# Sink attention and a mixture of attention experts in one program: three more rows are turned by way of DRAM, and the whole order is made anew

## The chip, the core and the metric

The program runs on one core of one Trainium2 chip. The core has a matrix engine (TensorE, here PE), a vector engine (DVE), a scalar engine (ACT), a general engine (POOL) and a queue engine (SP). They share an on-chip memory of 128 partitions (SBUF); PE writes into eight banks of PSUM. Each engine takes its own instructions in order and waits for others by semaphores. The metric is device time of one execution in microseconds (us). Before the change it is 361.75 us, the median of three runs (361.44 to 361.85).

## The reference

```python
def _attn_ref(q, k, v, n_sink, window):        # 4 batches, 8 heads, 768 positions, 64 wide
    scores = scale * np.matmul(q, k.transpose(0, 1, 3, 2))
    keep = is_sink | in_window                 # 4 first keys, and the last 128
    scores = np.where(keep, scores, -1e9)
    ...                                        # softmax over keys
    return np.matmul(a, v)

def _moe_ref(x, w_gate, wq, wk, wv, wo):       # x: heads side by side, 512 wide; 4 experts
    logits = x @ w_gate                        # the best 2 of 4 experts weigh in
    for e in range(E):
        q, k, v = x @ wq[e], x @ wk[e], x @ wv[e]
        scores = np.where(causal, -1e9, scale * (q @ k.transpose(0, 2, 1)))
        ...                                    # softmax over keys
        ye = a @ v @ wo[e]
        ...                                    # out += weight of the expert * ye
```

The first layer is attention in a band with four sinks; the second is full causal attention, once for each expert.

## The kernel before

**Units.** Heads are taken in pairs, and so are experts. A first-layer unit is one pair of heads of one batch (16 units), a second-layer unit one pair of experts of one batch (8 units). The 768 positions are six blocks of 128. Steps are named by batch, pair and layer: `001` is batch 0, pair 0, second layer (the unit of the change), `011` batch 0, pair 1, second layer, and `110` batch 1, pair 1, first layer. First-layer units of one batch are interleaved with the second-layer units of the batch before.

**One row of a second-layer unit.** Row i of six has the queries of block i and i + 1 key blocks. For each it runs: scores on PE (L1385, in `scores`); masking and a running minimum on DVE (L1602); exponentials with their sums on ACT (L1610); the reciprocal of the sum (L1445), times the expert's weight on POOL; scaling of the row (`norm` in `scaled`, L1256 or L1258). Then keys must come onto the partitions before the product with the values, that is, each 128x128 block of the row must be transposed. There are two ways:

- `transposed` (L1463 and following): PE transposes each block in halves of 64 (`turned`, L1457, into two PSUM banks), DVE or ACT copies the result from PSUM to a tile `pt` (`fn` in `evacuate`, L1247 on ACT, L1249 on DVE), and PE forms the product (L1424). Rows of five and six blocks go in two parts. A block takes four transpositions: two experts, two halves.
- `by_way_of_dram` (L1536 and following): the scaled row is written to a tile `u` with its columns rearranged; DVE turns blocks of 32x32 in two instructions (L1547); one DMA writes the tile to a buffer `there` in DRAM (L1550); four DMAs read it back with the blocks in their transposed places (L1554); PE forms the product from `u` (L1424). There are three tiles `u` and four buffers `there`.

`AWAY` names the units and the rows (3, 4 and 5, so rows of four, five and six blocks) that go the second way. In such a unit the rows are taken in the order 4, 5, 2, 3, 0, 1, since the groups of two are taken from the last.

**The order.** No engine's order is written by hand. `Plan.emit` lists all steps, with a cost of its own for each engine that could run the step, and places them one after the other. What stands on PE next follows from a priority (the unit's place, leads such as `WIDE_S`, and for each step a number from the table `NUDGE`), a price for a change of PE's mode (`STAY`, `BULK`) and for waiting (`HURRY`). `ONLY` fixes the engine of steps that could run on two. Loads, writes and reads back go to SP's queue in the same way. Where the planner finds PE without work in the first part of the program, it adds matrix instructions on zeros that nobody reads (`fill`, L1054 and L1057).

Of the kernel before, what the change touches and what calls it, by code (L numbers as in the profile page):

```python
# [34 lines left out]
for other in ("ROWS", "FULL", "cols", "rows"):  # L35
# [783 lines left out]
    "311 store_SPACT 3": SP, "311 fn_DVEACT 20": ACT, "311 fn_DVEACT 21": DVE, "311 store_SPACT 5": SP,  # L819
}  # L820

HURRY = 71.82
STAY = 104.82
BULK = -0.39
# [1197 lines left out]
```

## Time and profile before

| | us |
|---|---|
| median of three runs | 361.75 |
| profiled execution | 361.39 |
| its span, first to last instruction | 359.7 |
| PE busy | 351.2 |
| PE loading weights | 307.1 |
| DVE busy | 290.6 |
| ACT busy | 278.7 |
| POOL busy | 183.2 |

PE is counted in two rows, matrix instructions and loads of weights, which overlap. Its granted clock is 0.998 of full speed over the span, at the higher of its two levels. The page reports 52.05 MB moved by DMA. A busy PE means that some matrix instruction is under way; the gaps between kinds of instructions, in which one ends and the next has not begun to stream, are inside the busy time.

### The profile page before, as it was taken

Reading aid. Unit: us, or ns where it says so; the run is one execution under the profiler, and the core shown is the slowest. Engines: PE = TensorE matmul, PEld = TensorE weight load, DVE = VectorE, ACT = ScalarE, POOL = GpSimd, SP = SyncE. Lnnn points to the kernel's source line nnn. Section 1 sums busy time; section 2 is a strip of 40 time slices with the busy share of each in tenths; the row PEclk is TensorE's granted clock in tenths of the full one; section 3 lists DMA queues with packets and bytes.
Section 4 is the critical chain, followed back from the end, with each engine's and each line's share of the span. In section 5 each row is a group of like instructions: output and inputs, shape, how many; then the busy total and the mean of one; then the engine's idle time right before and its main releaser. Section 6 shows DMA issues by size and latency. Waiting matters only on the chain.

```text
span 359.7 us, 13333 instructions
## 1 busy us (share of the span) xinstructions
PE 351.2 (98%) x4822; PEld 307.1 (85%) x4822; DVE 290.6 (81%) x1263; ACT 278.7 (77%) x985; POOL 183.2 (51%) x432
## 2 busy tenths in 40 slices
PE   8989999999999999999999999999999999999995
PEld 7877789998888889978888888978898889988884
DVE  4899989599979979649799987489699875587951
ACT  2899999299998899758898977489899956056931
POOL 4298999778276764334646550153558600150420
PEclk9999999999999999999999999999999999999999
DMA  7877787943550798329787595029800463059313
GB/s 200 214 178 144 149 165 142 173 77 84 92 87 3 234 263 156 58 88 307 207 159 124 162 283 122 11 87 352 218 7 4 145 223 76 14 201 300 103 58 118
DMA packets 130849, 52.05 MB, mean 145 GB/s; under 512 B 109728, under 2 KB 125088, under 8 KB 130784
## 3 DMA queue, kind: packets, MB, share of 16 engines
q1 hardware_dynamic: 118336, 46.23, 52.0%
q10 hardware_dynamic: 12448, 4.98, 5.3%
q8 instruction: 38, 0.62, 0.8%
q14 instruction: 27, 0.22, 0.2%
HBM read 32.84 MB, written 18.09 MB: 142 GB/s over the span
## 4 chain that ended last, share of the span: by engine, by line
PE 80%; ACT 7%; DMA 4%; DVE 3%; POOL 3%; issue 2%; SPq 0%; ACTq 0%; POOLq 0%; DVEq 0%
PE b L1424 19%; PE b L1839 17%; PE b L1913 10%; PE b L1866 9%; PE b L1385 8%; PE b L1457 7%; PE b L1398 5%; PE b L1380 2%; DMA u<-there 2%; ACT p L1610 2%; PE b L1924 1%; ACT p L1740 1%; DMA there<-u 1%; PE b L1428 1%; DMA vn<-in_v_dram 1%
## 5 line engine op out<-in xcount | busy, mean ns | idle before, releaser
L1610 ACT ACTIVATE p<-p,st 128x256 f32<-128x256 f32 (+5 forms) x96 | 63.6, 665 | 9.8 <-DVE st L1602 9.6
L1740 ACT ACTIVATE p<-p,st 128x132 f32<-128x132 f32 x128 | 51.3, 406 | 3.2 <-DVE st L1736 3.1
L1602 DVE CUSTOM_DVE_ANT_0 p<-b,cmask 128x384 f32<-128x384 f32 (+3 forms) x96 | 45.7, 502 | 1.9 <-PE b L1385 1.5
L1247 ACT ACTIVATE pt<-b 128x256 f32<-128x256 f32 (+3 forms) x101 | 38.5, 419 | 7.5 <-PE b L1457 7.3
L1385 PE MATMUL b<-ks,qs 64*128 64x384 f32 (+3 forms) x384 | 42.2, 338 | 0.0
L1424 PE MATMUL b<-pt,vn 128*64 128x128 f32 x448 | 39.0, 280 | 0.3 <-ACT pt L1247 0.3
L1866 PE MATMUL b<-wvh,x 128*128 128x260 f32 x192 | 36.9, 285 | 0.0
L1440 POOL TENSOR_TENSOR st<-st 128x2 f32<-128x2 f32 (+1 forms) x47 | 9.3, 197 | 52.7 <-ACT p L1610 36.1
L1457 PE MATMUL b<-ident,p 64*128 64x64 f32 x760 | 36.0, 226 | 0.0
L1457 PEld LDWEIGHTS b<-ident,p 64*128 64x128 f32 x760 | 30.4, 138 | 5.4 <-issue 2.5
L1385 PEld LDWEIGHTS b<-ks,qs 64*128 64x128 f32 x384 | 31.6, 186 | 3.3 <-issue 0.7
L1839 PE MATMUL b<-x,wqh 128*128 128x256 f32 (+1 forms) x128 | 32.8, 343 | 0.0
L1839 PE MATMUL b<-x,wkh 128*128 128x256 f32 (+1 forms) x128 | 32.5, 340 | 0.0
L1913 PE MATMUL b<-woh,y 128*128 128x512 f32 x96 | 32.2, 402 | 0.0
L1753 POOL TENSOR_TENSOR p<-p,st 128x528 f32<-128x528 f32 x23 | 24.5, 1066 | 15.0 <-DVE st L1445 10.8
L1547 DVE STREAM_TRANSPOSE u<-u 128x640 f32<-128x640 f32 (+2 forms) x36 | 28.5, 824 | 4.0 <-ACT u L1256 3.7
L1736 DVE CUSTOM_DVE_ANT_0 p<-b,pair_mask 128x132 f32<-128x132 f32 x128 | 31.6, 286 | 0.1
L1679 ACT ACTIVATE p<-p,st 128x256 f32<-128x256 f32 (+1 forms) x64 | 29.1, 460 | 2.9 <-DVE st L1674 2.8
L1866 PEld LDWEIGHTS b<-wvh,x 128*128 128x128 f32 x192 | 30.4, 188 | 0.7 <-issue 0.3
L1249 DVE COPY pt<-b 128x256 f32<-128x256 f32 (+3 forms) x63 | 27.5, 453 | 2.6 <-PE b L1457 2.5
L1424 PEld LDWEIGHTS b<-pt,vn 128*64 128x64 f32 x448 | 25.1, 136 | 4.6 <-issue 1.7
L1866 PE MATMUL b<-wvl,x 128*128 128x260 f32 x96 | 27.1, 282 | 0.0
(133 smaller groups left out, 998.8 us busy)
## 6 DMA issues: line engine op xcount, KB each, us to landing
vn<-in_v_dram SPq DMA_DIRECT2D x24, 192.0 KB, 3.3
kn<-in_k_dram SPq DMA_DIRECT2D x48, 96.0 KB, 2.5
there<-u SPq DMA_DIRECT2D x6, 768.0 KB, 4.8
u<-there SPq DMA_DIRECT2D x24, 192.0 KB, 4.6
...
```

The lines of the kernel that those rows point to most:

```text
L1247: nc.scalar.activation(dst(), src(), AF.Copy)
L1385: nc.tensor.matmul(o, self.qs.t[hs, a, qs], keys(hs, b), start=n == 0, stop=n == 2)
L1424: nc.tensor.matmul(o[e * 64:e * 64 + 64], lhs, rhs, start=e not in self.begun, stop=last and self.done == len(self.steps))
L1457: nc.tensor.transpose(t[g].t[:, n, :], x[gs], ident[gs, gs])
L1602: nc.vector.tensor_tensor_reduce(out=one(e)[:, cs], in0=s2[e].t[:, :(c1 - c0) * 128], in1=mask(c0, c1), scale=times, scalar=st.t[:, 3, es] ...
L1610: nc.scalar.activation(x, x, AF.Exp, bias=st.t[:, 0, es], scale=-1.0, accum_out=st.t[:, 1, es])
L1679: nc.scalar.activation(x, x, AF.Exp, bias=st.t[:, 0, n:n + 1], scale=-1.0, accum_out=st.t[:, 1, n:n + 1])
L1736: nc.vector.tensor_tensor_reduce(out=p.t[:, n, :], in0=s2[e].t[:, 248 * r:248 * r + SW], in1=pair_mask, scale=-scale, scalar=BIG, op0=OP.a ...
L1740: nc.scalar.activation(p.t[:, n, :], p.t[:, n, :], AF.Exp, bias=st.t[:, 0, n:n + 1], scale=-1.0, accum_out=st.t[:, 1, n:n + 1])
L1839: nc.tensor.matmul(t.t, w[a][:, c, es], X[b, c].t[:, x, cs], start=c == 0 and m == 0, stop=c == NCH - 1 and m == 2)
L1866: nc.tensor.matmul(t.t[:, :VW], X[b, c].t[:, a, qs], W["wv"][w][:, c, :], start=c == 0 and n == 0, stop=c == NCH - 1 and n == 2)
L1913: nc.tensor.matmul(t.t, Y[b, c].t[:, a, qs], W["wo"][w][:, c, :], start=c == 0 and n == 0, stop=c == EP - 1 and n == 2)
```

## The change

Unit `001` joins the list `AWAY`, so that seven of the eight second-layer units send rows 3, 4 and 5 by way of DRAM. The tables `NUDGE` and `ONLY` and three numbers of the planner are replaced by others, so the order on every engine is a new one. The rest of the code is unchanged; its line numbers grow by 23 (L1457 becomes L1480, L1424 becomes L1447, L1547 becomes L1570).

```diff
 NUDGE = {
-    "busy_PE": 2.7, " ": -0.4, " busy_PE": 50.2, " busy_PE 0": 4.1, "sink_values_DVE": 20.3, " sink_values_DVE": 16.0,
...
+    "busy_PE": 7.4, " ": 1.2, " busy_PE": 8.1, " busy_PE 0": -44.6, " sink_values_DVE 0": -263.0, "load_SP": 245.1,
...
-HURRY = 71.82
-STAY = 104.82
-BULK = -0.39
+HURRY = 94.43
+STAY = 152.46
+BULK = -142.08
...
-    AWAY, MOVE = {u: (3,4,5) for u in ((0, 1), (1, 0), (1, 1), (2, 0), (2, 1), (3, 0))}, 250
+    AWAY, MOVE = {u: (3,4,5) for u in ((0, 0), (0, 1), (1, 0), (1, 1), (2, 0), (2, 1), (3, 0))}, 250
```

Over the whole program PE has 3413 instructions where it had 3457: 60 fewer of L1457 and 16 more of L1057. SP issues 3 more writes to `there` and 12 more reads back.

On PE, the products of unit `001` before: the rows of two parts and of four blocks from `pt`, then the transpositions of the next part. (`v_0_83` are the values of batch 0; `p_86` and `p_87` are one row of five blocks, one tile for each expert of the pair; `b` are PSUM banks.)

```order
L1380 MATMUL b_129<-kx_81,qn_65 128x256
L1424 MATMUL b_125<-pt_103,v_0_83 64x128 x6
L1424 MATMUL b_125<-pt_104,v_0_83 64x128 x8
L1424 MATMUL b_126<-pt_105,v_0_83 64x128 x6
L1457 MATMUL b_130<-ident,p_87 128x64
L1457 MATMUL b_128<-ident,p_87 128x64
L1457 MATMUL b_130<-ident,p_86 128x64
L1457 MATMUL b_128<-ident,p_86 128x64
L1457 MATMUL b_130<-ident,p_87 128x64
L1457 MATMUL b_128<-ident,p_87 128x64
```

The products of the same unit in the new order, behind the last band scores of the first-layer unit `130` and all projections of unit `011`:

```order
L1421 MATMUL b_125<-kx_82,qn_67 64x2x64
L1421 MATMUL b_129<-kx_82,qn_67 64x2x64
L1447 MATMUL b_127<-u_94,v_0_83 64x128 x10
L1447 MATMUL b_126<-pt_105,v_0_83 64x128 x6
L1447 MATMUL b_127<-u_95,v_0_83 64x128 x12
L1480 MATMUL b_128<-ident,psk_109 128x64
L1480 MATMUL b_130<-ident,psk_109 128x64
```

The rows of five and six blocks now come from `u`, in one block of 10 and one of 12, and the transpositions of their blocks are gone; those that follow belong to a first-layer unit.

On SP, ahead of the first writes to DRAM. Before, the queue at this place holds loads alone, and the first write is that of unit `011`:

```order
L1800 DMA vn_71<-in_v_dram 128x6x64 x2
L1800 DMA vn_70<-in_v_dram 128x6x64 x2
L1804 DMA qn_67<-in_q_dram 32x24x32 x4
L1804 DMA kn_69<-in_k_dram 32x24x32 x4
L1804 DMA qn_65<-in_q_dram 32x24x32 x4
L1804 DMA kn_69<-in_k_dram 32x24x32 x4
L1800 DMA vn_72<-in_v_dram 128x6x64 x2
L1550 DMA there_99<-u_94 128x1280
```

In the new order the first write is that of unit `001` (1280 columns are the row of five blocks, 1536 of six, 1024 of four):

```order
L1827 DMA kn_69<-in_k_dram 32x24x32 x4
L1823 DMA vn_72<-in_v_dram 128x6x64 x2
L1573 DMA there_99<-u_94 128x1280
L1823 DMA vn_71<-in_v_dram 128x6x64 x2
L1577 DMA u_94<-there_99 32x4x320 x4
L1573 DMA there_100<-u_95 128x1536
L1573 DMA there_101<-u_96 128x1024
L1827 DMA qn_66<-in_q_dram 32x24x32 x4
L1577 DMA u_95<-there_100 32x4x384 x4
L1577 DMA u_96<-there_101 32x4x256 x4
```

Two loads of values and one of queries stand among the three writes and their ways back.

On DVE, in the new order, the first two turns of unit `001` (`x` and `cmask` rows are the first layer's output and the masked minimum of scores; ISA is how the order names the latter):

```order
L1625 ISA p_90,st_121<-b_129,cmask,st_121 128x384
L1625 ISA st_121 128x1
L1570 STREAM_TRANSPOSE u_94<-u_94 128x640
L1272 CAST sk_111<-b_130 64x64
L1258 SCALAR_TENSOR_TENSOR x_79<-b_126,x_79 128x256
L1272 CAST sk_111<-b_131 64x64
L1570 STREAM_TRANSPOSE u_94<-u_94 128x640
L1468 RECIPROCAL st_121<-st_121 128x2
```

They stand among the minimum, the copies for the sinks and the split of the first layer's output; four more follow within the next forty rows.

## Rows read from the trace of the kernel before

**Rows 1.** The page: its head, and the busy time of each engine in us, with the share of the span and the number of instructions.

```profile
span 359.7 us, 13333 instructions
...
PE 351.2 (98%) x4822; PEld 307.1 (85%) x4822; DVE 290.6 (81%) x1263; ACT 278.7 (77%) x985; POOL 183.2 (51%) x432
```

**Rows 2.** The table by stretches of the span: length, then busy us and (in brackets) instructions of PE, of PE's weight loads, of DVE, ACT and POOL, then granted clock, share of the transfer engines, GB/s.

```profile
0.00:50.00 50.00, 46.41 (x1013) 38.94 (x1014) 43.72 (x236) 41.18 (x173) 35.90 (x83) 1.00 0.78 175
...
73.00:96.00 23.00, 23.00 (x434) 20.56 (x435) 22.28 (x109) 22.19 (x74) 15.03 (x35) 1.00 0.39 73
96.00:131.00 35.00, 34.97 (x416) 30.27 (x407) 31.25 (x128) 31.75 (x122) 22.91 (x54) 1.00 0.56 138
...
170.00:212.00 42.00, 42.00 (x516) 36.39 (x517) 38.19 (x166) 37.59 (x143) 26.32 (x61) 1.00 0.77 181
```

**Rows 3.** The waits of PE: its line, what it waited for, us in total, times, the longest.

```profile
PE b L1424 <- DMA u<-there: 0.8, 1, 0.8
PE b L1398 <- POOL kx L1322: 0.7, 1, 0.7
PE b L1457 <- POOL psk L1759: 0.6, 1, 0.6
PE b L1424 <- ACT pt L1247: 0.3, 1, 0.3
```

**Rows 4.** The chain that ended last, in order of time: start, length, what, how many.

```profile
54.01 1.67 PE b L1398 x40
...
96.37 8.73 PE b L1839 x48
...
107.00 1.17 PE b L1457 x32
...
136.19 4.85 PE b L1424 x84
...
178.40 0.86 PE b L1380 x8
...
187.33 0.93 PE b L1385 x12
```

**Rows 5.** The timeline of PE from 73.4 to 96.4 us: start, length, line, what it writes and reads, shapes, how many. Lengths of neighbours overlap; the starts tell the pace.

```profile
78.99 0.39 PE L1424 MATMUL b<-pt,vn 128*64 128x128 f32 x4
79.21 0.39 PE L1424 MATMUL b<-pt,dv 128*64 128x128 f32 x4
79.53 0.28 PE L1457 MATMUL b<-ident,psk 64*128 64x64 f32 x2
...
82.84 0.59 PE L1457 MATMUL b<-ident,p 64*128 64x64 f32 x12
83.23 0.89 PE L1385 MATMUL b<-ks,qs 64*128 64x384 f32 x5
```

**Rows 6.** The same view from 5.5 to 13 us, around filling instructions (L1057).

```profile
10.24 0.88 PE L1057 MATMUL b<-nought 128*64 128x128 f32 x12
11.06 1.58 PE L1398 MATMUL b<-kx,qn 64*64 64x196 f32 x48
```

**Rows 7.** Groups of instructions, shapes kept apart, on DVE and on ACT: how many, busy us, mean ns of one, idle time before them.

```profile
L1249 DVE COPY pt<-b 128x256 f32<-128x256 f32 x33 | 13.4, 413 | 0.2 <-PE b L1457 0.2
L1249 DVE COPY pt<-b 128x384 f32<-128x384 f32 x23 | 12.4, 545 | 0.5 <-PE b L1457 0.5
L1547 DVE STREAM_TRANSPOSE u<-u 128x768 f32<-128x768 f32 x12 | 11.1, 951 | 0.9 <-ACT u L1256 0.9
L1547 DVE STREAM_TRANSPOSE u<-u 128x640 f32<-128x640 f32 x12 | 9.7, 828 | 2.5 <-ACT u L1256 2.5
...
L1547 DVE STREAM_TRANSPOSE u<-u 128x512 f32<-128x512 f32 x12 | 8.1, 692 | 0.6 <-POOL u L1258 0.3 <-ACT u L1256 0.3
...
L1247 ACT ACTIVATE pt<-b 128x256 f32<-128x256 f32 x51 | 18.6, 381 | 1.0 <-PE b L1457 0.9
L1247 ACT ACTIVATE pt<-b 128x384 f32<-128x384 f32 x37 | 17.0, 496 | 5.1 <-PE b L1457 4.9
...
L1247 ACT ACTIVATE pt<-b 128x512 f32<-128x512 f32 x3 | 1.7, 596 | 0.0
```

**Rows 8.** The timeline of PE at three rows that go by way of DRAM, each with its scores (L1385) and its product (L1424 from `u`): in unit `011` (115.91 and 138.58), in unit `111` (191.55 and 219.04) and in unit `211` (279.92 and 300.74). In brackets the idle time before, and what ended it.

```profile
115.91 0.96 PE L1385 MATMUL b<-ks,qs 64*128 64x512 f32 x6
...
138.58 2.47 PE L1424 MATMUL b<-u,v 128*64 128x128 f32 x40
...
191.55 1.45 PE L1385 MATMUL b<-ks,qs 64*128 64x384 f32 x12
...
219.04 1.53 PE L1424 MATMUL b<-u,v 128*64 128x128 f32 x24 [0.85 <-DMA u<-there]
...
279.92 1.11 PE L1385 MATMUL b<-ks,qs 64*128 64x512 f32 x7
...
300.74 1.09 PE L1424 MATMUL b<-u,v 128*64 128x128 f32 x16
```

**Rows 9.** The chain that ended last from 203 us, where it runs through transfers.

```profile
203.24 2.92 DMA vn<-in_v_dram
206.24 4.16 DMA there<-u
...
211.84 7.06 DMA u<-there
```

More of the change, by code (lines that the diff above doesn't have):

```diff
@@ L816 @@
[L816 to L824 removed]
+    " load_SPACT 1": SP, " load_SPACT 3": SP, " load_SPACT 6": SP, "000 load_SPACT 0": SP, "000 load_SPACT 1": SP,
@@ new lines @@
+    "000 load_SPACT 3": SP, "000 load_SPACT 4": SP, "000 fn_DVEACT 3": DVE, "000 fn_DVEACT 4": DVE, "000 fn_DVEACT 5": DVE,
+    "000 fn_DVEACT 6": ACT, "000 fn_DVEACT 7": DVE, "000 norm_POOLACT 0": ACT, "000 norm_POOLACT 1": POOL,
+    "000 fn_DVEACT 8": ACT, "000 fn_DVEACT 9": ACT, "000 total_DVEPOOL 1": DVE, "000 norm_POOLACT 2": ACT,
+    "000 fn_DVEACT 10": ACT, "000 fn_DVEACT 12": DVE, "000 fn_DVEACT 13": ACT, "000 fn_DVEACT 14": ACT,
+    "000 fn_DVEACT 15": ACT, "000 fn_DVEACT 16": ACT, "000 fn_DVEACT 17": DVE, "010 load_SPACT 0": SP,
@@ new lines @@
+    "010 load_SPACT 1": SP, "010 load_SPACT 2": SP, "010 fn_DVEACT 0": DVE, "010 fn_DVEACT 1": DVE, "010 fn_DVEACT 2": ACT,
+    "010 fn_DVEACT 3": DVE, "010 fn_DVEACT 4": DVE, "010 fn_DVEACT 5": ACT, "010 fn_DVEACT 6": DVE,
+    "010 total_DVEPOOL 0": DVE, "010 norm_POOLACT 0": ACT, "010 norm_POOLACT 1": POOL, "010 fn_DVEACT 8": ACT,
+    "010 fn_DVEACT 9": DVE, "010 fn_DVEACT 10": DVE, "010 fn_DVEACT 11": DVE, "010 fn_DVEACT 12": DVE,
+    "010 norm_POOLACT 3": ACT, "010 fn_DVEACT 17": DVE, "020 load_SPACT 0": SP, "020 load_SPACT 1": SP,
@@ new lines @@
+    "030 fn_DVEACT 6": DVE, "030 fn_DVEACT 7": ACT, "030 norm_POOLACT 0": ACT, "030 norm_POOLACT 1": POOL,
+    "030 fn_DVEACT 8": DVE, "030 total_DVEPOOL 1": POOL, "030 norm_POOLACT 2": ACT, "030 fn_DVEACT 11": DVE,
+    "030 fn_DVEACT 12": DVE, "030 total_DVEPOOL 2": POOL, "030 norm_POOLACT 3": POOL, "030 fn_DVEACT 14": ACT,
+    "030 fn_DVEACT 17": ACT, "110 load_SPACT 1": SP, "110 load_SPACT 2": SP, "110 norm_POOLACT 0": POOL,
+    "110 fn_DVEACT 0": DVE, "110 fn_DVEACT 1": DVE, "110 total_DVEPOOL 1": POOL, "110 fn_DVEACT 3": ACT,
@@ new lines @@
+    "110 fn_DVEACT 4": DVE, "110 fn_DVEACT 5": ACT, "110 fn_DVEACT 6": ACT, "110 fn_DVEACT 8": ACT, "110 fn_DVEACT 9": DVE,
+    "100 load_SPACT 1": SP, "100 total_DVEPOOL 0": DVE, "100 norm_POOLACT 0": POOL, "100 norm_POOLACT 1": ACT,
+    "100 fn_DVEACT 0": DVE, "100 total_DVEPOOL 1": DVE, "100 norm_POOLACT 2": ACT, "100 fn_DVEACT 2": DVE,
+    "100 fn_DVEACT 5": DVE, "100 norm_POOLACT 3": ACT, "100 fn_DVEACT 9": ACT, "001 fn_DVEACT 0": DVE,
+    "001 fn_DVEACT 2": ACT, "001 fn_DVEACT 3": DVE, "001 fn_DVEACT 4": ACT, "001 fn_DVEACT 5": ACT,
@@ new lines @@
+    "120 norm_POOLACT 0": ACT, "120 norm_POOLACT 1": POOL, "120 fn_DVEACT 0": ACT, "120 fn_DVEACT 1": DVE,
+    "120 total_DVEPOOL 1": DVE, "120 fn_DVEACT 3": ACT, "120 fn_DVEACT 4": DVE, "120 fn_DVEACT 5": DVE,
+    "120 norm_POOLACT 3": ACT, "120 fn_DVEACT 6": ACT, "120 fn_DVEACT 8": DVE, "120 fn_DVEACT 9": DVE,
+    "130 load_SPACT 0": SP, "130 load_SPACT 1": SP, "130 load_SPACT 2": SP, "130 total_DVEPOOL 0": POOL,
+    "130 norm_POOLACT 0": POOL, "130 fn_DVEACT 0": ACT, "130 fn_DVEACT 1": ACT, "130 norm_POOLACT 2": POOL,
@@ new lines @@
+    "130 total_DVEPOOL 2": POOL, "130 norm_POOLACT 3": POOL, "130 fn_DVEACT 7": ACT, "130 fn_DVEACT 9": ACT,
+    "011 total_DVEPOOL 0": POOL, "011 norm_POOLACT 0": POOL, "011 norm_POOLACT 2": POOL, "011 norm_POOLACT 3": ACT,
+    "011 norm_POOLACT 4": POOL, "011 norm_POOLACT 5": POOL, "011 fn_DVEACT 1": ACT, "011 norm_POOLACT 7": POOL,
+    "011 total_DVEPOOL 4": DVE, "011 norm_POOLACT 8": POOL, "011 norm_POOLACT 9": POOL, "011 fn_DVEACT 3": ACT,
+    "011 norm_POOLACT 10": POOL, "011 norm_POOLACT 11": POOL, "011 fn_DVEACT 5": DVE, "011 store_SPACT 0": ACT,
@@ new lines @@
+    "011 fn_DVEACT 8": ACT, "011 store_SPACT 2": SP, "011 fn_DVEACT 9": DVE, "011 store_SPACT 3": SP,
+    "011 fn_DVEACT 10": DVE, "011 store_SPACT 4": SP, "011 store_SPACT 5": SP, "210 load_SPACT 0": SP,
+    "210 load_SPACT 1": SP, "210 norm_POOLACT 0": POOL, "210 norm_POOLACT 1": POOL, "210 fn_DVEACT 0": ACT,
+    "210 fn_DVEACT 1": ACT, "210 norm_POOLACT 2": POOL, "210 fn_DVEACT 4": ACT, "210 fn_DVEACT 5": ACT,
+    "210 total_DVEPOOL 2": POOL, "210 norm_POOLACT 3": POOL, "210 fn_DVEACT 7": DVE, "210 fn_DVEACT 8": ACT,
@@ new lines @@
+    "200 load_SPACT 0": SP, "200 load_SPACT 1": SP, "200 total_DVEPOOL 0": DVE, "200 norm_POOLACT 0": ACT,
+    "200 fn_DVEACT 1": ACT, "200 total_DVEPOOL 1": DVE, "200 fn_DVEACT 2": ACT, "200 fn_DVEACT 3": ACT,
+    "200 fn_DVEACT 4": ACT, "200 fn_DVEACT 5": ACT, "200 total_DVEPOOL 2": DVE, "200 norm_POOLACT 3": POOL,
+    "200 fn_DVEACT 6": ACT, "200 fn_DVEACT 7": ACT, "200 fn_DVEACT 8": DVE, "101 fn_DVEACT 0": DVE, "101 fn_DVEACT 1": ACT,
+    "101 fn_DVEACT 2": DVE, "101 fn_DVEACT 3": ACT, "101 fn_DVEACT 5": ACT, "101 total_DVEPOOL 0": DVE,
@@ new lines @@
+    "101 norm_POOLACT 1": POOL, "101 norm_POOLACT 2": ACT, "101 norm_POOLACT 3": POOL, "101 total_DVEPOOL 2": DVE,
+    "101 norm_POOLACT 5": POOL, "101 norm_POOLACT 9": POOL, "101 total_DVEPOOL 5": DVE, "101 norm_POOLACT 10": ACT,
+    "101 fn_DVEACT 10": DVE, "101 fn_DVEACT 11": ACT, "220 load_SPACT 0": SP, "220 load_SPACT 1": SP,
+    "220 norm_POOLACT 0": ACT, "220 norm_POOLACT 1": POOL, "220 fn_DVEACT 0": DVE, "220 fn_DVEACT 1": ACT,
+    "220 norm_POOLACT 2": POOL, "220 fn_DVEACT 2": DVE, "220 fn_DVEACT 3": ACT, "220 fn_DVEACT 5": DVE,
@@ new lines @@
+    "111 norm_POOLACT 3": POOL, "111 total_DVEPOOL 2": DVE, "111 norm_POOLACT 4": ACT, "111 norm_POOLACT 5": ACT,
+    "111 fn_DVEACT 0": DVE, "111 total_DVEPOOL 3": POOL, "111 norm_POOLACT 7": POOL, "111 total_DVEPOOL 4": POOL,
+    "111 norm_POOLACT 9": POOL, "111 total_DVEPOOL 5": DVE, "111 norm_POOLACT 10": POOL, "111 norm_POOLACT 11": ACT,
+    "111 fn_DVEACT 4": ACT, "111 fn_DVEACT 5": DVE, "111 fn_DVEACT 6": DVE, "111 store_SPACT 0": SP,
+    "111 store_SPACT 1": SP, "111 fn_DVEACT 8": ACT, "111 fn_DVEACT 9": ACT, "111 fn_DVEACT 10": ACT,
@@ new lines @@
+    "111 store_SPACT 5": ACT, "300 load_SPACT 0": SP, "300 load_SPACT 1": SP, "300 load_SPACT 2": SP,
+    "300 total_DVEPOOL 0": DVE, "300 norm_POOLACT 0": ACT, "300 fn_DVEACT 0": ACT, "300 fn_DVEACT 1": DVE,
+    "300 total_DVEPOOL 1": DVE, "300 norm_POOLACT 2": POOL, "300 fn_DVEACT 3": ACT, "300 fn_DVEACT 5": ACT,
+    "300 total_DVEPOOL 2": POOL, "300 norm_POOLACT 3": ACT, "300 fn_DVEACT 7": DVE, "300 fn_DVEACT 9": DVE,
+    "201 fn_DVEACT 2": ACT, "201 fn_DVEACT 3": DVE, "201 fn_DVEACT 4": ACT, "201 fn_DVEACT 5": DVE,
@@ new lines @@
+    "310 fn_DVEACT 1": DVE, "310 norm_POOLACT 2": POOL, "310 fn_DVEACT 2": DVE, "310 fn_DVEACT 3": ACT,
+    "310 total_DVEPOOL 2": DVE, "310 fn_DVEACT 6": DVE, "310 fn_DVEACT 7": ACT, "310 fn_DVEACT 8": DVE,
+    "310 fn_DVEACT 9": DVE, "320 load_SPACT 0": SP, "320 load_SPACT 1": SP, "320 total_DVEPOOL 0": DVE,
+    "320 norm_POOLACT 0": POOL, "320 norm_POOLACT 1": POOL, "320 fn_DVEACT 1": ACT, "320 total_DVEPOOL 1": DVE,
+    "320 norm_POOLACT 2": POOL, "320 fn_DVEACT 2": DVE, "320 fn_DVEACT 3": DVE, "320 fn_DVEACT 4": ACT,
@@ new lines @@
+    "211 norm_POOLACT 3": POOL, "211 total_DVEPOOL 2": DVE, "211 norm_POOLACT 4": ACT, "211 norm_POOLACT 5": POOL,
+    "211 fn_DVEACT 0": ACT, "211 norm_POOLACT 6": POOL, "211 norm_POOLACT 7": ACT, "211 norm_POOLACT 9": POOL,
+    "211 norm_POOLACT 10": POOL, "211 norm_POOLACT 11": POOL, "211 fn_DVEACT 5": DVE, "211 fn_DVEACT 7": ACT,
+    "211 store_SPACT 1": SP, "211 store_SPACT 2": ACT, "211 store_SPACT 3": ACT, "211 fn_DVEACT 10": DVE,
+    "211 store_SPACT 4": ACT, "211 fn_DVEACT 11": ACT, "211 store_SPACT 5": ACT, "301 fn_DVEACT 0": DVE,
@@ new lines @@
+    "301 fn_DVEACT 1": DVE, "301 fn_DVEACT 3": ACT, "301 fn_DVEACT 4": ACT, "301 fn_DVEACT 5": DVE,
+    "301 total_DVEPOOL 1": DVE, "301 norm_POOLACT 2": ACT, "301 norm_POOLACT 3": POOL, "301 total_DVEPOOL 2": POOL,
+    "301 norm_POOLACT 4": POOL, "301 norm_POOLACT 5": POOL, "301 fn_DVEACT 6": ACT, "301 fn_DVEACT 7": ACT,
+    "301 total_DVEPOOL 3": DVE, "301 norm_POOLACT 6": POOL, "301 norm_POOLACT 7": POOL, "301 total_DVEPOOL 4": DVE,
+    "301 norm_POOLACT 9": POOL, "301 fn_DVEACT 8": ACT, "301 fn_DVEACT 9": ACT, "301 norm_POOLACT 10": POOL,
@@ new lines @@
+    "301 norm_POOLACT 11": ACT, "301 fn_DVEACT 10": ACT, "311 fn_DVEACT 0": ACT, "311 total_DVEPOOL 1": POOL,
+    "311 norm_POOLACT 2": POOL, "311 norm_POOLACT 3": ACT, "311 fn_DVEACT 2": ACT, "311 fn_DVEACT 3": ACT,
+    "311 total_DVEPOOL 2": POOL, "311 norm_POOLACT 4": ACT, "311 fn_DVEACT 5": ACT, "311 total_DVEPOOL 3": DVE,
+    "311 fn_DVEACT 7": DVE, "311 total_DVEPOOL 4": POOL, "311 norm_POOLACT 8": ACT, "311 norm_POOLACT 9": ACT,
+    "311 fn_DVEACT 10": DVE, "311 fn_DVEACT 11": DVE, "311 total_DVEPOOL 5": DVE, "311 norm_POOLACT 11": POOL,
```

139 lines of the change are left out of this document (37 added, 102 removed), and 1347 rows, old and new, of the table NUDGE.

## The prediction

> **What bounds the kernel now.** I read the page's head and its busy times first, then the table by stretches, then the waits of TensorE (PE), then the chain that ended last. The reader is to see in the head that PE is busy 351.2 of 359.7 us [rows 1]: its idle time is 8.5 us in all, so whatever shortens this kernel must take instructions or gaps away from PE. The table shows where others come near it: from 73 to 96 us, where the first second-layer unit of batch 0 runs, PE is busy all 23.00 us, DVE 22.28 and ACT 22.19; from 96 to 131 us DVE has 31.25 of 35 [rows 2]. So in the very place of the change three engines are full, and work may leave PE only if it does not land on a full one. The first 50 us have 3.6 us of idle PE (50 less 46.41), from the start and the first loads, which the change does not shorten. The waits of PE that the profile names are small: the longest that a finished start-up leaves is 0.8 us, for a transfer back from DRAM [rows 3].
>
> **The change, part by part.** The sum is made against the profiled execution, 361.39 us (span 359.7 and 1.69 around it), which lies 0.36 under the median of 361.75.
>
> *Sixty transpositions leave PE.* Rows of four, five and six blocks have 16, 20 and 24 instructions of L1457. In the chain 32 of them took 1.17 us, 36.6 ns each [rows 4]; a block of twelve that was followed by scores began at 82.84 and its successor at 83.23, 32.5 ns each [rows 5]. At 36.6 the sixty are 2.2 us; at 32.5 they are 1.95. I take 2.2, because the larger block holds the gaps between blocks too. The products stay: sixty instructions of L1424, now with `u` as operand instead of `pt`, in three blocks instead of joined parts. A page of the Trainium skill speaks against this step: "VectorE: DVE Perf Modes", section "Rules for kernel authors", advises TensorE for a 128x128 transposition that may go to PSUM. By that rule the 2.2 us would not be gained at all; the rows above say what TensorE pays, and those of DVE below what replaces it, so the rule's case is the rival on DVE.
>
> *Switches between kinds of work on PE.* Counted over the whole program by the form of the block, PE changes between product, score, transposition, band and full-width blocks 210 times before and 217 after. Nine more are from a transposition to scores, and the others fall by two. From one group of four products to the next it is 0.22 us (78.99 to 79.21), and from such a group to a transposition 0.32 (79.21 to 79.53) [rows 5], so a dear change costs about 0.10. From transpositions to scores the twelve above show next to nothing. Nine at 0.02 to 0.03 are 0.2 us, my value; the bounds are 0 and seven at 0.10, 0.7.
>
> *Filling instructions.* L1057 goes from 28 to 44, all in the first 45 us or so of work. Six such instructions (12 rows in the trace) hold 0.82 us, from 10.24 to 11.06 [rows 6]. Sixteen more are 2.2 us if nothing covers them. They stand where PE would otherwise wait, and the first 50 us have 3.6 us of idle PE besides [rows 2], so I take 0; the upper bound is 2.2.
>
> *Copies out of PSUM go, turns come.* Ten copies disappear. Before, the order has eight of them on ACT (two of 512 columns, five of 384, one of 256) and two on DVE (256 and 384). By their rows that is 4.05 us less on ACT and 0.96 less on DVE [rows 7]. DVE gains six turns: twice 692, 828 and 951 ns, 4.94 us. Net, DVE has 3.98 us more. DVE's idle time is 0.72 us from 73 to 96 and 3.75 from 96 to 131 [rows 2], 4.47 together: the turns fit, with half a microsecond to spare, if they may slide into the later stretch. They may, as their products stand behind the next unit's projections. I take 0.2 us for a wait of PE on DVE; the bounds are 0 and 3.98 less 0.72, 3.3, if all of it falls where DVE has no room. In DVE's favour the copies are needed by the next product at once, and the turns are not.
>
> The rows of that stretch also show the share in which PE loads weights: 20.56 of 23, 89%, below DVE's 97% [rows 2]. The Trainium skill, "Perfetto Trace Analysis", section "Identifying the Most-Contended Engine", says that matmul busy time is no measure of how close PE is to its limit, that the share of weight loads is better, and that the engine with the highest occupancy is the one to relieve. By that rule DVE bounds the stretch and the change costs up to the 3.3 us; by PE's row of 23.00 the sum stands as above. The trace does not decide between them, so it is the slower rival.
>
> *Transfers.* SP gets three writes and twelve reads back more, and the rows' products wait for them. What hides them is the PE work between a row's scores and its product. In the order after, 48 projections (8.73 us), 48 band scores (40 rows of the trace in 1.67, so 96 in 4.0), 30 scores (12 in 0.93, so 2.3), 54 products (108 rows at 4.85 over 84, 6.2), 44 transpositions (1.6) and sixteen rows of L1380 (0.86 for eight, 1.7) stand between the scores and the product of the row of six blocks, with eight instructions on the sinks beside [rows 4]: about 24 us. For the row of four it is 22, for that of five 24. What such a cover is worth is measured. From 115.91 to the last sixteen of the forty products that begin at 138.58 it was some 24 us with no wait; from 279.92 to 300.74 20.8 with none; from the second half of the block at 191.55 to 219.04 27, with a wait of 0.85 [rows 8]. That one came because SP's queue held the write from 203.24 to 206.24 behind a load of `v`, and the way back then took 7.06 us [rows 9]. In the order after, a load of `vn` stands on SP just ahead of the unit's first write and another between that write and the way back, so the same can happen. One in four of the short covers waited: a third of a chance for each of the three new ones, rounded up, at 0.85 is 0.6 us with a little to spare below it. The bounds are 0 and three times 0.85, 2.6.
>
> *The order made anew.* Every other block of the program moves too. For that the trace before has no row. The waits of PE that the profile names after the start (0.8, 0.7, 0.6, 0.3 and less) add up to about 3 us [rows 3]; a new order could save most of them or make as many again. I take 0, with bounds of 2.8 either way.
>
> Sum: -2.2 + 0.2 + 0 + 0.2 + 0.6 + 0 = -1.2 us, so 360.2 as a profiled execution and 360.5 as a median. The bounds of the parts about the change itself are -2.2 (nothing lost) and +6.6 (every loss at once).
>
> **The rivals.** (1) *The order finds PE's waits too.* All of the 2.2 us comes through, and of the named waits some 2 us go: 361.75 - 4.2 = 357.5. For it: the waits have several releasers, POOL, ACT and DMA, so order alone can move them. Against it: the new table fills 16 instructions more in the first stretch, where it sees idle PE, and that tells of no saving there.
>
> (2) *Transfers late: the saving is eaten.* Two of the three new products wait as at 219.04, or one waits and an old one does: 2.2 less 1.7, less 0.4 for switches and DVE, leaves 0.1: 361.65. For it: SP takes its instructions in order, and a load that waits for PE holds the writes behind it. Against it: in 73 to 96 us the transfer engines are busy 39% only, against 77% from 170 to 212 where the late one started [rows 2].
>
> (3) *DVE becomes the engine waited for (slower).* Place: the first unit's softmax, 73 to 96 us. Price: the turns that fall there, 3.98 - 0.72 = 3.3 us, and PE's saving becomes waiting: 361.75 + 3.3 = 365.0 at full price, 363 when nearly half of it falls there. It decides from the point where PE waits for DVE for more than 1.8 us (the 2.2 that its transpositions save, less 0.4 for switches and one short late transfer). For it: 97% of DVE, and the rule above. Against it: ACT loses 4 us there, and copies may be moved from DVE to ACT.
>
> (4) *The new order loses elsewhere.* New waits of some 2.5 us against 1.2 saved: 363.0. It needs no change of the first unit at all; what speaks for it is that ten rows by way of DRAM, by the same count of the blocks between scores and product, have at most 26 us of cover, against four before, of which one waited.
>
> That the change does nothing is excluded: the sixty transpositions are gone from PE's order.
>
> **How the numbers follow.** This kernel's measurement tells about 0.2%, 0.7 us, from no change: faster is below 361.0, slower above 362.5. My forecast, 360.5 with its own range of 359.2 to 361.5, has 0.44, of which 0.08 lies within 0.2%. Rival 1 has 0.17, all faster. Rival 2 has 0.16, of which 0.12 is within 0.2%, 0.02 faster and 0.02 slower. Rival 3 has 0.11 and rival 4 0.12, both slower but for 0.02. Faster: 0.36 + 0.17 + 0.02 = 0.55; within: 0.08 + 0.12 + 0.02 = 0.22; slower: 0.02 + 0.11 + 0.10 = 0.23. The range for eight in ten goes from 357.4, which takes in rival 1, to 363.4, which takes in rivals 2 and 4 and the lower half of rival 3.
>
> **What would show it.** In the profile after: L1480, the transposition's new line number, with 60 instructions fewer and its busy time less by about 2 us or more; six more turns on DVE; among PE's waits one or two for the way back of about 0.8 us, and none above 1.5. Rival 3 shows as DVE at 99% in the stretch of the first unit with PE idle on DVE; rival 1 as idle PE of 6 us or less in the whole span, where it was 8.5; rivals 2 and 4 as 9 to 11. I am wrong if PE's idle time and its gaps between blocks change by more than its sixty instructions are worth: then the order, and not the transpositions, decides the result.

## The result, and the profile after

The changed kernel takes 365.75 us (median of four runs, 364.73 to 368.23); the kernel before, beside it on the same chip, 361.62 (361.44 to 361.85). The ratio is 1.0134, with an interval of 1.0106 to 1.0162: slower by 4.1 us by the medians and 4.8 by the ratio, where 1.2 us faster was forecast, and outside the range. The profiled execution after is one of 366.69 us.

The head of its page answers to [rows 1]: PE is busy 354.2 of 365.0 us, so 10.8 us idle where it was 8.5.

```profile
span 365.0 us, 13320 instructions
...
PE 354.2 (97%) x4794; PEld 309.0 (85%) x4794; DVE 294.5 (81%) x1280; ACT 273.4 (75%) x960; POOL 186.6 (51%) x439
```

The table by stretches answers to [rows 2], with the same columns. From 73 to 96 us PE had no idle time before and has 2.23 us now, the granted clock, the last column but two, is 0.93 on the mean, and DVE is *less* busy than before (21.49 for 22.28). No engine is full there any more.

```profile
0.00:50.00 50.00, 47.92 (x1050) 40.53 (x1050) 43.20 (x237) 41.14 (x170) 33.88 (x82) 1.00 0.76 172
73.00:96.00 23.00, 20.77 (x258) 17.31 (x257) 21.49 (x84) 17.79 (x55) 16.06 (x36) 0.93 0.51 119
96.00:131.00 35.00, 34.71 (x502) 30.33 (x502) 34.13 (x153) 32.90 (x129) 20.11 (x51) 1.00 0.85 207
170.00:212.00 42.00, 41.12 (x579) 35.59 (x576) 38.79 (x170) 35.20 (x135) 23.57 (x55) 1.00 0.78 186
```

The waits of PE answer to [rows 3]. The two for transfers are small, as forecast. New at the head is a wait of the scores (L1408) for `qs` and `ks`, written by DVE at L1333.

```profile
PE b L1408 <- DVE qs L1333: 1.7, 1, 1.7
PE b L1447 <- DMA u<-there: 1.4, 2, 0.8
PE b L1947 <- DVE lanes L1133: 1.1, 1, 1.1
PE b L1421 <- DVE ks L1333: 0.9, 1, 0.9
PE b L1408 <- DVE ks L1333: 0.5, 1, 0.5
```

Where it stands is told by the timeline of PE. The first scores of unit `001` begin at 74.48, and the second instruction of the block only at 76.61.

```profile
74.26 0.41 PE L1480 MATMUL b<-ident,p 64*128 64x64 f32 x8
74.48 0.42 PE L1408 MATMUL b<-ks,qs 64*128 64x384 f32 x1
76.61 0.44 PE L1408 MATMUL b<-ks,qs 64*128 64x384 f32 x1 [1.71 <-DVE qs L1333]
77.54 0.62 PE L1408 MATMUL b<-ks,qs 64*128 64x384 f32 x4 [0.49 <-DVE ks L1333]
...
78.27 1.84 PE L1408 MATMUL b<-ks,qs 64*128 64x256 f32 x12
79.90 0.86 PE L1480 MATMUL b<-ident,p 64*128 64x64 f32 x12
80.50 1.32 PE L1408 MATMUL b<-ks,qs 64*128 64x384 f32 x6
81.61 0.45 PE L1451 MATMUL b<-sk,vs 64*128 64x128 f32 x2
```

DVE's timeline just ahead shows why, and that DVE was not overloaded. It stands idle for 2.89 us before two turns of `qn` (L1378), whose load has not landed. Those turns belong to a first-layer unit, `130`, that needs them later; behind them in DVE's queue are the gate (L1920 to L1924) and the residuals (L1333) that PE wants at once.

```profile
70.20 0.20 DVE L1468 RECIPROCAL st<-st 128x4 f32<-128x4 f32 x2
73.29 1.04 DVE L1378 STREAM_TRANSPOSE qn<-qn 128x384 f32<-128x384 f32 x2 [2.89 <-DMA qn<-in_q_dram]
74.25 0.57 DVE L1920 SCALAR_TENSOR_TENSOR gate<-gate 128x24 f32<-128x24 f32 x1
...
75.88 1.01 DVE L1333 TENSOR_TENSOR qs<-b,qs 128x512 fp32r<-128x512 f32 x2
76.81 1.01 DVE L1333 TENSOR_TENSOR ks<-b,ks 128x512 fp32r<-128x512 f32 x2
```

In the kernel before the same queue has the residuals of `ks` ahead of a turn of `qn`, and that turn does not wait for its load:

```profile
70.62 0.98 DVE L1310 TENSOR_TENSOR ks<-b,ks 128x512 fp32r<-128x512 f32 x2
71.53 1.02 DVE L1355 STREAM_TRANSPOSE qn<-qn 128x384 f32<-128x384 f32 x2
72.79 1.02 DVE L1310 TENSOR_TENSOR qs<-b,qs 128x512 fp32r<-128x512 f32 x2 [0.24 <-ACT qs L1307]
```

The chain that ended last carries the delay one step further back: the load of `qn` runs behind a load of `vn` that SP issues first.

```profile
66.21 4.19 DMA vn<-in_v_dram
...
70.42 2.75 DMA qn<-in_q_dram
...
73.79 0.54 DVE qn L1378
...
75.95 0.93 DVE qs L1333 x2
76.88 0.61 DVE ks L1333
```

The stall has a second part. In the table by single microseconds the granted clock is full (2.4 GHz) while PE stands, and falls to 0.50 (1.2 GHz) right after it, in 78 to 82 us, when PE is busy all the time again.

```profile
75.00:76.00 1.00, 0.00 (x0) 0.00 (x0) 0.90 (x5) 0.19 (x2) 0.92 (x4) 1.00 1.11 177
76.00:77.00 1.00, 0.39 (x1) 0.18 (x1) 1.00 (x3) 0.00 (x0) 1.00 (x2) 1.00 1.04 166
77.00:78.00 1.00, 0.51 (x6) 0.43 (x7) 1.00 (x3) 0.00 (x0) 0.29 (x1) 1.00 0.02 3
78.00:79.00 1.00, 1.00 (x20) 1.00 (x18) 1.00 (x5) 0.69 (x4) 0.24 (x1) 0.71 0.00 0
79.00:80.00 1.00, 1.00 (x11) 0.92 (x10) 1.00 (x5) 0.45 (x3) 0.40 (x1) 0.50 0.00 0
80.00:81.00 1.00, 1.00 (x18) 1.00 (x16) 0.65 (x4) 1.00 (x3) 0.51 (x1) 0.50 0.00 0
81.00:82.00 1.00, 1.00 (x10) 0.93 (x6) 1.00 (x4) 0.82 (x3) 0.33 (x2) 0.59 0.07 16
```

So the theory (A) is: the new order put a turn with a late load at the head of DVE, ahead of what PE needs. Its rivals are the seventh unit's route by DRAM itself (B), a clock that fell by chance (C), and small losses elsewhere (D, E). Letters that an expectation explains otherwise have the meaning given there.

### The profile page after: what moved, and what is told of

It reads as the page before. It is cut to its first block, busy times and chain, and to the rows that moved or that the text cites. A ratio compares the mean times of both kernels' runs of the same rounds, so it can differ in the third digit from the quotient of the medians.

```text
span 365.0 us, 13320 instructions
## 1 busy us (share of the span) xinstructions
PE 354.2 (97%) x4794; PEld 309.0 (85%) x4794; DVE 294.5 (81%) x1280; ACT 273.4 (75%) x960; POOL 186.6 (51%) x439
## 4 chain that ended last, share of the span: by engine, by line
PE 63%; ACT 10%; DVE 10%; DMA 9%; issue 3%; POOL 2%; SPq 2%; DVEq 0%; POOLq 0%; ACTq 0%
PE b L1447 15%; PE b L1936 9%; PE b L1889 9%; PE b L1862 9%; PE b L1408 8%; PE b L1480 6%; DMA u<-there 4%; DMA qn<-in_q_dram 3%; PE b L1421 3%; ACT p L1763 2%; ACT p L1702 2%; PE b L1403 2%; ACT p L1633 1%; DVE p L1625 1%; PE b L1947 1%
## 5 line engine op out<-in xcount | busy, mean ns | idle before, releaser
L1633 ACT ACTIVATE p<-p,st 128x512 f32<-128x512 f32 (+5 forms) x96 | 63.7, 665 | 10.3 <-DVE st L1625 7.2
L1408 PE MATMUL b<-ks,qs 64*128 64x384 f32 (+3 forms) x384 | 44.4, 346 | 2.2 <-DVE qs L1333 1.7
L1270 ACT ACTIVATE pt<-b 128x256 f32<-128x256 f32 (+2 forms) x95 | 36.1, 415 | 8.0 <-PE b L1480 4.8
L1447 PE MATMUL b<-pt,vn 128*64 128x128 f32 x448 | 39.1, 280 | 0.1
L1408 PEld LDWEIGHTS b<-ks,qs 64*128 64x128 f32 x384 | 32.6, 192 | 5.1 <-DVE qs L1333 2.0
L1480 PE MATMUL b<-ident,p 64*128 64x64 f32 x700 | 35.4, 228 | 0.0
L1570 DVE STREAM_TRANSPOSE u<-u 128x640 f32<-128x640 f32 (+2 forms) x42 | 33.5, 825 | 1.3 <-ACT u L1279 1.1
L1480 PEld LDWEIGHTS b<-ident,p 64*128 64x128 f32 x700 | 29.8, 140 | 5.5 <-issue 2.1
L1702 ACT ACTIVATE p<-p,st 128x128 f32<-128x128 f32 (+1 forms) x64 | 29.0, 458 | 5.9 <-DVE b L1751 3.3
L1862 PE MATMUL b<-x,wqh 128*128 128x512 f32 (+1 forms) x128 | 32.9, 343 | 0.0
L1862 PE MATMUL b<-x,wkh 128*128 128x512 f32 (+1 forms) x128 | 32.5, 341 | 0.0
L1421 PE MATMUL b<-kx,qn 64*64 64x68 f32 (+2 forms) x768 | 27.0, 276 | 1.2 <-DVE ks L1333 0.9
L1447 PE MATMUL b<-u,v 128*64 128x128 f32 x420 | 26.7, 275 | 1.5 <-DMA u<-there 1.4
L1447 PEld LDWEIGHTS b<-pt,vn 128*64 128x64 f32 x448 | 25.4, 136 | 3.0 <-ACT pt L1270 0.5
```

The costliest lines, as they stand in the source:

```text
L1270: nc.scalar.activation(dst(), src(), AF.Copy)
L1408: nc.tensor.matmul(o, self.qs.t[hs, a, qs], keys(hs, b), start=n == 0, stop=n == 2)
L1421: nc.tensor.matmul(o, self.q_of()[hs, q0 + 64 * h:q0 + 64 * h + 64], ks, start=True, stop=True)
L1447: nc.tensor.matmul(o[e * 64:e * 64 + 64], lhs, rhs, start=e not in self.begun, stop=last and self.done == len(self.steps))
L1480: nc.tensor.transpose(t[g].t[:, n, :], x[gs], ident[gs, gs])
L1633: nc.scalar.activation(x, x, AF.Exp, bias=st.t[:, 0, es], scale=-1.0, accum_out=st.t[:, 1, es])
```

## Experiments

No run exchanges the route and the order one by one. Instead the changed kernel's plan is frozen in all kernels but one, and single steps are moved in the finished list, before the instructions are written out. In the shape of a diff, with the moves of the first run:

```diff
+        for name, side, other in (
+            ("130 turn_DVE 0", "behind", "001 low_DVE 3"),
+            ("130 turn_DVE 2", "behind", "130 turn_DVE 0"),
+        ):
...
+            order.insert(at[other] + (side == "behind"), moving)
         for _, _, s in order:
```

A step's name is its unit, its function, the engines it may use and a number: "001 low_DVE" are steps that write residuals. Below, only the moved steps are given, and the expectations stand in the order of the runs. Ratios are to the kernel before on the same chip.

**The turn and its load.** In the second run the two turns "330 turn_DVE" 2 and 0 also go behind "111 low_DVE 1", for the wait of L1421 at 186 us (0.88 us for `ks`, among the waits of PE).

> The changed kernel with its plan frozen; only the two turns of qn of the first layer's unit 130 are emitted behind the four residuals (L1333) of the second-layer unit 001 instead of ahead of them on DVE. Theory A (the new order: DVE stands 2.89 us before a turn whose load is late, the residuals queued behind it come late, TensorE idles 2.2 us at 74 to 78 us, and its granted clock is then at half for 3.4 us, about 1.7 us more): 361.9 us (361 to 363), clock 1.0 in 73 to 96 us, TensorE's wait for qs and ks at L1408 there under 0.5 us. Theory B (the seventh unit's route by DRAM itself, its turns and transfers): DVE has as much to do, so the wait only moves: 365 to 366.5 us. Theory C (the clock fell by chance, not by the idle time): about 363.5 us with the half-clock stretch still in some profile.

> As the run before, and also the two turns of qn of unit 330 emitted behind the residual pieces of unit 111 that stand behind them at 184 to 187 us. Theory A: both stalls were turns whose loads are late, so another 1.2 to 1.4 us is gone: 360.5 us (359.5 to 362), under the kernel before. Theory B: 365 to 366.5 us.

The first: 1.0046 (1.0026 to 1.0066), 362.62 us, so 3.2 us of the 4.8 are gone, the clock is 1.00 in 73 to 96 us, and the wait for `ks` and `qs` there is 0.16 us. The second: 1.0051 (1.0026 to 1.0076), no further gain where 1.2 to 1.4 us were expected. Its PE waits for copies of `pt` instead (0.9 us), as the turns now stand ahead of those on DVE.

Then the load itself, on SP, with the order of the turns on DVE untouched: earlier, and later. The changed kernel ran again beside the later load.

```diff
+            ("130 load_SPACT 0", "ahead", "110 load_SPACT 2"),
```
```diff
+            ("130 load_SPACT 0", "behind", "210 load_SPACT 1"),
```

> The changed kernel with its plan frozen; on SP the load of qn of unit 130 is issued ahead of the load of vn of unit 110 instead of behind it (1.2 us earlier, and its packets ahead of vn's). Theory A: the turn waits 1.2 to 2.5 us less, the stall at 74 us shrinks from 2.2 us to 0 to 1 us and the clock stays or falls for less time: 362 to 364.5 us. Theory B: nothing of the seventh unit's route changes: 365 to 366.5 us.

> The changed kernel as it is, once more, beside the three kernels of this group on one chip. All theories: 1.0134 of the kernel before, some 365 to 366.5 us; more of its runs than of the others with a granted clock under 0.998.

> The changed kernel with the suspected cost made larger: the load of qn of unit 130 is issued on SP behind the first load of kn of unit 210 instead of ahead of it, some 2 us later. Theory A: DVE stands 2 us longer before that turn, and TensorE with it, and the clock falls in every run: 2 to 3.5 us above the changed kernel of the same group, 367.5 to 369.5 us, half clock for 3 us or more in the profile. Theory B (the turn's wait is not the price): within 0.7 us of the changed kernel.

Earlier: 1.0043 (1.0016 to 1.0071). The changed kernel again: 1.0127 (1.0096 to 1.0159). Later: 1.0201 (1.0178 to 1.0224), 368.30 us against 365.39 beside it, 2.9 us more. In the run with the later load, DVE's timeline has at that turn:

```profile
74.36 1.04 DVE L1385 STREAM_TRANSPOSE qn<-qn 128x384 f32<-128x384 f32 x2 [5.46 <-DMA qn<-in_q_dram]
```

Its timeline of PE, at the second score of the block:

```profile
77.34 0.69 PE L1415 MATMUL b<-ks,qs 64*128 64x384 f32 x1 [3.71 <-DVE qs L1340]
```

And its table by stretches:

```profile
73.00:96.00 23.00, 19.05 (x237) 15.90 (x238) 20.16 (x76) 15.61 (x48) 13.57 (x28) 0.85 0.43 102
76.00:82.00 6.00, 4.42 (x41) 3.84 (x41) 5.18 (x19) 1.86 (x7) 0.74 (x2) 0.50 0.01 2
```

DVE's idle time before that turn went from 2.89 to 5.46 us, PE's wait from 1.71 to 3.71, and the time up by 2.9. With the load earlier the wait and the half clock are gone. The timeline of PE in that run:

```profile
73.86 1.06 PE L1415 MATMUL b<-ks,qs 64*128 64x384 f32 x6
...
75.17 1.13 PE L1415 MATMUL b<-ks,qs 64*128 64x256 f32 x12
76.14 0.53 PE L1487 MATMUL b<-ident,p 64*128 64x64 f32 x12
76.48 0.78 PE L1415 MATMUL b<-ks,qs 64*128 64x384 f32 x6
77.10 0.33 PE L1458 MATMUL b<-sk,vs 64*128 64x128 f32 x2
```

The same blocks, from the first score to the product of the sinks, take 3.24 us here (73.86 to 77.10) and 7.13 in the changed kernel (74.48 to 81.61). The difference of 3.9 us is 2.2 of waiting (1.71 and 0.49) and 1.7 of slower work behind it, 1.4 of them between 78.27 and 81.61. Theory A is shown for this stall: order and load each remove it, and a later load makes it larger. C falls too: the clock is at 0.995 or less in all six runs of the changed kernel again and all six with the later load, but in only two of the twenty in which the turns alone or the load alone went to a better place (0.994 each). The second profile of the changed kernel shows the same chain, with 1.0 and 0.5 us of waiting at the scores.

**The route by DRAM.** Unit `001`'s transfers are left out, first in the changed kernel, then with the earlier load; last its six turns of `u` on DVE too. These three kernels leave out the exchange, so their products are not those of the reference; they only price it. The diff is that of the last.

```diff
+            if s.part and s.part[2] in ("001 turn_DVE", "001 by_way_of_dram_SP", "001 back_SP"):
+                continue
             s.fn()
```

> The changed kernel without the six transfers groups (to DRAM and back) of the three rows of unit 001; the turns, the products and everything else stay. It leaves out the exchange through DRAM, so those rows are multiplied untransposed between partition groups. Theory A: the stall at 74 to 78 us comes before the first of these transfers and stays; only TensorE's waits for u (0.97 us at 141 us is another unit's; at most 0.3 to 0.6 us here) can go: 364.5 to 366 us. Theory B: the transfers are the price: 361 to 362.5 us.

> The run with qn of unit 130 loaded ahead of vn, without unit 001's six groups of transfers to DRAM and back; those rows are multiplied without the exchange. It prices the seventh unit's transfers where the stall at 74 us no longer covers anything. Theory of the prediction (transfers late, 0.6 us, at most 2.6): 1.0043 less 0.0017, 1.0026 of before (0.998 to 1.0045). Theory B (the transfers are what is left): 0.9985 or less.

> As the run without unit 001's transfers, and its six turns of u on DVE are left out too (4.9 us less of DVE's work, at 82 to 96 us). If DVE's added work costs (the prediction's third rival): 1.5 to 3 us under the run without the transfers. If DVE has room, as the prediction's sum took it (0.2 us): within 0.7 us of it.

Without transfers: 1.0075 (1.0048 to 1.0101), between what the theories gave and some 2 us under the changed kernel. The stall stays but is shorter in the profile, the fastest of five executions: PE waits 0.6 and 0.5 us for `qs` and `ks` at the scores, with the clock at 1.00; in the other four the clock is 0.993 to 0.995. With the earlier load and no transfers: 1.0016 (0.9991 to 1.0041), 1.0 us under the same kernel with them (1.0043). Without the turns too: 1.0026 (1.0010 to 1.0043), nothing gained. So the transfers cost about 1 us where the stall is gone, by the intervals anything from nothing to over 2, and 4.9 us of turns on DVE cost nothing that can be measured. Theory B explains no more of the loss than this.

**The sixty transpositions.** The opposite edit prices the saving: 60 are added where unit `001` still turns a row on PE, in the kernel before and in the changed one with the earlier load.

```diff
-            for m in range(n):
-                turned(t, m, block(m % 2, m // 2))
+            for k in range(6 if part == "001" and i == 2 else 1):
+                for m in range(n):
+                    turned(t, m, block(m % 2, m // 2))
```

> The kernel before with 60 transpositions more on TensorE: the last of unit 001's narrow rows is turned six times instead of once (same result). It prices the first term of the prediction in the old order. If TensorE is full there: 2.2 us more, 1.006 of before (1.0045 to 1.0075). If it waits there anyway: 1.000 to 1.002.

> The run with qn of unit 130 loaded ahead of vn, and 60 transpositions put back on TensorE: the last of unit 001's rows that TensorE still turns is turned six times instead of once (same result). Theory A (the saving of the 60 transpositions is real and whole, the stalls merely hid it): 2.2 us above the same kernel without them, 1.0104 of before (1.0085 to 1.012). Theory C (in the new order TensorE waits at that place anyway, so they cost nothing there and saved nothing): 1.0043 to 1.006.

In the kernel before: 1.0057 (1.0036 to 1.0078), 2.1 us. In the new order: 1.0061 (1.0041 to 1.0081) against 1.0043, 0.65 us. The intervals overlap, so that difference is not exact, but 1.0061 lies under the 1.0085 to 1.012 that theory A gave for a whole saving. The profiles show why the sixty can be cheaper here. Without them PE waits twice for rows on their way back from DRAM, once in unit `001` and once in `011`:

```profile
103.54 1.53 PE L1454 MATMUL b<-u,v 128*64 128x128 f32 x24 [0.70 <-DMA u<-there]
138.75 1.09 PE L1454 MATMUL b<-u,v 128*64 128x128 f32 x16 [0.56 <-DMA u<-there]
```

With the sixty put back it does not wait at either product: the work put back covers these transfers, and the kernel that saves it waits instead. That is one execution of each, and which part of the 1.5 us it explains was not tried.

**What is left.** On top of the earlier load, the following steps were moved: the return from DRAM ahead of a load (first run); two products with `u` later on PE (second); these and the turns of unit `330` much later (third); all of it (fourth).

```diff
+            ("200 load_SPACT 0", "behind", "001 back_SP 1"),
+            ("200 turn_DVE 0", "ahead", "200 turn_DVE 2"),
```
```diff
+            ("001 av_PE 1", "behind", "011 go_PE 1"),
+            ("011 av_PE 2", "behind", "210 tr_PE 0"),
+            ("330 turn_DVE 2", "ahead", "300 turn_DVE 1"),
+            ("330 turn_DVE 0", "ahead", "300 turn_DVE 1"),
```

> The run with qn of unit 130 loaded ahead of vn (1.0043 of before), and also the return from DRAM of the second row of unit 001 issued ahead of the load of qn of unit 200 on SP, with the first turn of that qn put off on DVE. Theory A: what that run still lost against before is in small waits, the largest TensorE's 0.87 us for u of unit 001 at 102 us: 0.5 to 0.9 us of it goes, 1.002 of before (0.9995 to 1.0045). Theory B (the waits for u are covered elsewhere, something after takes the time up): 1.0043 or more.

> The run with qn of unit 130 loaded ahead of vn (1.0043 of before), and two products with u put later on TensorE: the second of unit 001 behind the scores of 011 that follow it, the last of unit 011 behind the next first-layer transpositions. Theory A (what is left over before is TensorE standing for u from DRAM, 0.87 us at 102 and 0.73 us at 137 us): 1 to 1.5 us less, 1.000 to 1.0015 of before. Theory D (the waits are only the place where a chain that is late anyway shows): 1.003 or more.

> The run with the earlier load of qn of unit 130 and the two later products with u (1.0024 of before), and besides the two turns of qn of unit 330 put off on DVE behind the first-layer work of unit 230 that follows them. Theory A (the stall at 181 to 187 us, 1.1 to 2.2 us of TensorE in the runs so far, is again a turn whose load is late at the head of DVE): 1 to 2 us less, 0.997 to 1.000 of before. Theory E (that stall comes from the residuals and copies themselves, with or without the turns): 1.0015 to 1.004, and TensorE still loses over 1 us between the first-layer scores of unit 230 at 181 to 187 us.

> The same, with the return of unit 001's second row from DRAM also issued ahead of the load of qn of unit 200 (its first turn put off). Theory A: another 0 to 0.5 us. If the return's place does nothing any more, since the product with it was put later: the same as the run beside it.

They gave 1.0031 (1.0011 to 1.0050), 1.0024 (1.0007 to 1.0041), 1.0015 (0.9999 to 1.0031) and 1.0022 (1.0002 to 1.0042). Each step is small, and the intervals overlap; together they bring the kernel to within 0.2% of before, not under it. In the first run the wait of the second row is gone, but the third row of the same unit waits 0.80 us instead. The second gains 0.7 us where its theory A gave 1 to 1.5. In the third the named wait for `ks` at 181 to 187 us is gone, yet the time lies at the edge of theory E's range and not in A's. The waits of PE in the third run, start-up included:

```profile
PE b L1958 <- DVE lanes L1144: 1.1, 1, 1.1
PE b L1458 <- DMA u<-there: 0.4, 1, 0.4
PE b L1432 <- ACT kx L1281: 0.4, 1, 0.4
```

Last, the fills. In that third kernel each group was made one pair of products shorter, which gives before's 28, or all were left out (0 in place of n - 1).

```diff
-        for _ in range(n):
+        for _ in range(n if mode == "FULL" else n - 1):
```

> The run with all three repairs (qn of 130 earlier, products with u later, turns of 330 later; 1.0015 of before), with each group of fills on TensorE one pair of products shorter: 28 of them as in the kernel before, instead of 44 (1.7 us of TensorE's busy time less). If the new plan's 16 more fills cost what they last (the prediction took 0, bound 2.2): 0.8 to 1.7 us less, 0.997 to 0.9995 of before. If they lie in TensorE's idle time: 1.000 to 1.003.

> The same with none of these fills (44 fewer than in the run with all three repairs). If fills cost what they last: about twice to three times the effect of the run beside it. If they keep the granted clock up: slower, with a granted clock under 1.0 somewhere in the first 50 us of the profile. If neither: the same as the run with all three repairs.

Both are slower than the 1.0015: 1.0057 (1.0037 to 1.0076) and 1.0089 (1.0060 to 1.0118). Without fills the granted clock falls, as the second reading in that run's expectation had it; its table by stretches:

```profile
10.00:14.00 4.00, 3.33 (x138) 2.83 (x130) 3.55 (x22) 3.10 (x14) 0.00 (x0) 1.00 0.90 217
14.00:18.00 4.00, 3.05 (x38) 2.60 (x40) 2.73 (x17) 3.18 (x13) 2.46 (x7) 0.58 0.74 196
```

With fewer fills the clock stays at 1.00 in the profile, and the wait for `ks` at the band scores is back with 1.2 us. Why is not settled: a shift of a microsecond at the start changes which transfers meet later.

## Why the prediction was wrong

The step that failed is *the order made anew*, taken at 0 with bounds of 2.8 either way. Its bounds were the named waits of PE before [rows 3], and a wait of an order that is not yet there has no row among them. It measured about 5 us: 4.1 of loss by the medians, and the 2.1 that the transpositions save in the old order, less 1.0 for the transfers and 0.4 for switches and DVE as forecast, make 4.8; by the ratio it is 5.5. If the sixty save only 0.65 us in the new order, it is some 1.5 less, 3.4 to 4.0, still outside the bounds. Of it the stall at 74 us is 3.9 by its rows and 3.2 to 3.3 by the runs that remove it: a load that lands late, a turn that waits for it at the head of DVE's queue, the residuals behind that turn, and half the clock afterwards.

*Sixty transpositions, -2.2.* Right in the old order, 2.1 us. In the new order one comparison gives 0.65, so the old order's price may not hold there. The sign given for it in the profile did not come: L1480 is busy 35.4 us for 700 where it was 36.0 for 760. Instructions that overlap are counted once there, so 60 fewer need not show by what they cost; the 700 also stand in 78 blocks where the 760 stood in 72, and some ran at half clock. The group in the page after:

```profile
L1480 PE MATMUL b<-ident,p 64*128 64x64 f32 x700 | 35.4, 228 | 0.0
```

Before:

```profile
L1457 PE MATMUL b<-ident,p 64*128 64x64 f32 x760 | 36.0, 226 | 0.0
```

*Fills, 0.* No cost is seen: with 16 fewer of them the kernel is slower. *Copies and turns, +0.2.* DVE is busy 3.9 us more, as worked out (3.98), and taking 4.9 us off it changes nothing. Rival 3, DVE as the engine that bounds, is refuted as a load, though PE does wait for DVE: 2.2 us, past the 1.8 that it named. The waiting engine stood idle itself, for a transfer. With the earlier load DVE is busy 22.91 of 23 us from 73 to 96, and PE 22.98, so it does not hold PE back. By the Trainium skill, "Perfetto Trace Analysis", section "Identifying the Most-Contended Engine", the busiest engine is the one to relieve; the run without the turns does not agree for DVE (DVE is busy 18.80 us from 73 to 96 instead of 22.84, and the ratio is 1.0026 instead of 1.0016). *Transfers, +0.6.* The size came, 1.0 us by the runs, and partly by luck: the two waits in the profile after, 0.80 and 0.58 us, are at 142.96 and 224.56, in other units, and the second stood before with 0.85 [rows 8]. The three new products do not wait in that profile; the one at 103.54 does once the stall is gone. *Switches, +0.2.* Not tried apart.

Rival 4 was right in kind: it needs no change of the first unit, and 10.8 us of idle PE lie within its 9 to 11. It was too small, with 2.5 us of new waits, as it did not reckon with the clock behind a wait. And what it gave for itself, rows by way of DRAM with too little cover, is not what came: the stall is a turn with a late load, and it lies ahead of the first of unit `001`'s transfers. The sign of no wait above 1.5 us failed with it (1.71). The last sentence of the prediction, that the order and not the transpositions decides if idle time and gaps change by more than these are worth, is what came.

Open is where the rest of the saving goes. With everything mended the kernel should be 1.2 us faster by the terms and is level (1.0015). The cheaper transpositions of the new order are one candidate. Another is waiting inside the busy time: in the profile of the third run of *What is left* PE has 1.7 us less idle time than before (6.8 for 8.5) but is busy 1.2 us more (352.4 for 351.2), with sixty transpositions fewer and sixteen fills more; after the first 50 us, where the fills end, it is busy 304.5 for 304.8 us. A block of 48 band scores in that run, and one of 48 before:

```profile
180.21 2.61 PE L1432 MATMUL b<-kx,qn 64*64 64x196 f32 x48
```
```profile
94.73 1.64 PE L1398 MATMUL b<-kx,qn 64*64 64x196 f32 x48
```

Between its weight loads the first has waits of 0.4 us for `ks` and 0.4 for `pt`, at a granted clock of 1.00, and PE counts as busy throughout. What such waits add up to was not measured.
